# The first unit of a fused attention and MoE kernel under a fixed engine order

## The chip, the cores and the metric

One of the eight cores of a Trainium2 chip runs the whole program. The metric is device time in microseconds (us) from the start to the end of one execution; lower is better. Below, PE is TensorE (PEld its weight loads), DVE is VectorE, ACT is ScalarE, POOL is GpSimd, SP is SyncE, and L12 is line 12 of the kernel's file.

## What is computed

Three stages follow each other on 4608 tokens: an attention through 32 packed queries per head, a dense MLP with squared ReLU, and a routed MLP of eight experts.

```python
def _attn_ref(q, k, v, p):                 # q, k, v: 8 x 8 x 576 x 64, p: 8 x 8 x 32 x 64
    p_packed = sm_attn(p, k, v)            # packs: softmax(p k^T) v
    return sm_attn(q, p_packed, p_packed)  # the tokens attend to the packs

def _moe_ref(x, w_in, w_out):              # w_in 512 x 2048, w_out 2048 x 512, given as float64 words
    h = np.maximum(x @ w_in, 0.0)
    return h * h @ w_out

def _moe2_ref(x, modality_id, w_gate, modality_bias, w1, w2):
    logits = x @ w_gate + modality_bias[modality_id]
    ...                                    # each token goes to its best expert, scaled by its gate
```

## The kernel before

**The pack phase** (steps `i` = 0 to 18 of a loop written out under `tc.manual_schedule()`, so that every engine takes its instructions in the written order). Step `i` works on quad `i`, four heads of a batch: `scores(i)` on PE, `greatest(i)` (maximum on DVE, exponential on ACT), `normalise(i)`, then two steps later the transposes (`turn_a`, `turned_a`), and three steps later `values(i - 3)` and `packs(i - 3)`. `packs` reads the result `pq` out of PSUM twice, on DVE into `pp32` (the operand of the tokens' attention) and on ACT into `ppq` (a compact copy), in turn for each half. Beside it run, one piece per step, the conversion of the float64 weights (`conv_in` for w_in, four DVE instructions and one ACT square per block; `conv_out` for w_out, which also halves the result into a high and a low part on ACT and POOL), `turn_p` on POOL, which makes the left operand of `scores` two batches ahead, and from step 11 the quads `pw_quad`: the packs times w_in, two matmuls of 64 rows each, copied out of PSUM into `pws` and written to `pw_d` in DRAM. One quad is 512 KB. Sixteen of the 32 are made in the steps, for batches 0 to 3. `att2(0)`, the attention of the first 384 tokens, runs in nine pieces in steps 10 to 18.

**The units.** The tokens go through the dense MLP in twelve units of 384 tokens. Unit `u` loops over 16 blocks `f` of the hidden width: `layer1` (6 matmuls into `ph`; ACT: ReLU, square, high part; the low part of `ghl` on POOL in unit 0 and on DVE later) and `layer2` of the block before (9 matmuls into `acc`). The left operand of `layer1` are blocks of `pw_d`, loaded (`load_pw`, into `praw`) and halved by `split_pw` on ACT and POOL into `head` and `ring`. Unit 0 carries more (`others`): the other 16 quads, `conv_out` of the last 12 blocks of w_out, and `att2(1)`; the constants of the routing (`setup_routing`, some 30 small POOL instructions and two small loads) also belong to it in the code. Unit 1 begins with `tail(0)`, the router's dot products of unit 0 on DVE.

**What sets the order.** Only the pack phase stands under the manual schedule. From there on a scheduler orders each engine's instructions by its own estimate of when they can run, and it may lift an instruction of a later part above the end of the pack phase. All loads and some of the writes are issued by SP, in order; writes of `pws` copied by ACT in the pack phase are issued by ACT. PSUM is eight banks; `pws` has three buffers, `praw` two.

Of the kernel before, what the change touches and what calls it, by code (L numbers as in the profile page):

```python
# [26 lines left out]
def tile_pack_attention_moe_moe2(  # L27
# [880 lines left out]
    with tc.manual_schedule():  # L908
# [58 lines left out]
        for w in (2, 3):
            split_pw(0, w - 1)
            for _ in conv_out(w):
                pass  # L970
        split_pw(0, 3)
    st2.close()
    ps0.close()
    held.pop("early")
# [150 lines left out]
```

## Time and profile before

| | us |
|---|---|
| median of 3 runs | 1281.64 (1280.64 to 1284.12) |
| the profiled execution, its own time | 1284.8 |
| its span, first to last instruction | 1282.9 |
| PE busy in the span | 1214.0 (95%) |
| DVE busy | 835.7 (65%) |
| ACT busy | 637.6 (50%) |
| POOL busy | 293.7 (23%) |
| mean granted TensorE clock | 0.985 |

Busy shares are means over the whole span. A stage is read from a window of its own, from the timeline (start, duration, engine, line, operation, what it writes and reads, and in brackets the idle time of the engine before it and what ended that idle time), and from groups of instructions within a window.

### The profile page before, as it was taken

How to read it: one execution, taken by the hardware profiler on the slowest of the kernel's cores; microseconds unless marked ns; L12 is line 12 of the kernel's file. 1: busy time of each engine (PE TensorE's matmuls, PEld its weight loads, DVE VectorE, ACT ScalarE, POOL GpSimd, SP SyncE). 2: the span in 40 equal slices, each digit the busy share in tenths (PEclk: the TensorE clock that was granted, in tenths of full speed). 3: DMA queues.
4: the chain of work that ended last, by engine and by line, in shares of the span. 5: the costliest groups of instructions: out<-in, count | busy, mean ns of one | idle time of the engine just before them, and what ended most of it. 6: DMA issues, size and time to landing. Idle time of an engine off the chain costs nothing.

```text
span 1282.9 us, 17702 instructions
## 1 busy us (share of the span) xinstructions
PE 1214.0 (95%) x6036; PEld 982.3 (77%) x6036; DVE 835.7 (65%) x2145; ACT 637.6 (50%) x1328; POOL 293.7 (23%) x353
## 2 busy tenths in 40 slices
PE   6886799999999999999999998999999999999995
PEld 4653456788888888888888887878788888888884
DVE  5766964968767984878778497878653354354331
ACT  4664564676546766466755576632332343243220
POOL 5013733322103232013320033101221122032011
PEclk8998899999999999999999999999999999999998
DMA  9988754221111212112110112341442452353210
GB/s 338 366 331 270 225 201 158 64 75 66 35 42 50 75 50 67 43 30 87 59 58 17 51 51 76 103 145 68 157 156 91 150 182 94 121 193 116 88 66 35
DMA packets 75316, 149.20 MB, mean 116 GB/s; under 512 B 5712, under 2 KB 25296, under 8 KB 75088
## 3 DMA queue, kind: packets, MB, share of 16 engines
q1 hardware_dynamic: 66464, 123.04, 28.5%
q0 software_dynamic: 5760, 19.17, 4.6%
q10 hardware_dynamic: 2992, 5.77, 1.2%
q8 instruction: 49, 0.80, 0.3%
q14 instruction: 51, 0.42, 0.1%
HBM read 112.01 MB, written 35.95 MB: 115 GB/s over the span
## 4 chain that ended last, share of the span: by engine, by line
PE 71%; DVE 15%; DMA 6%; ACT 3%; issue 3%; POOL 2%; ACTq 0%; POOLq 0%; SPq 0%; DVEq 0%
PE acc L519 23%; PE h L809 15%; PE o L831 15%; PE ph L493 9%; DVE rows L540 5%; PE pw L376 2%; DMA wraw<-in_moe_w 2%; PE s L444 2%; DVE r L506 1%; PE tr L789 1%; DVE ghl L512 1%; DMA wgb<-in_k 1%; DMA pw_d<-pws 1%; PE pq L354 1%; DMA early<-in_v 1%
## 5 line engine op out<-in xcount | busy, mean ns | idle before, releaser
L519 PE MATMUL acc<-wb,ghl 128*128 128x512 f32 x1728 | 445.8, 400 | 9.5 <-ACT ghl L510 8.3
L519 PEld LDWEIGHTS acc<-wb,ghl 128*128 128x128 f32 x1728 | 318.6, 189 | 81.3 <-ACT ghl L510 11.3
L540 DVE SCALAR_TENSOR_TENSOR rows<-rows,wgb 128x512 f32<-128x512 f32 x288 | 213.8, 742 | 3.6
L809 PE MATMUL h<-xt,wb 128*128 128x512 f32 x864 | 213.9, 397 | 0.5 <-DVE ht L820 0.5
L809 PEld LDWEIGHTS h<-xt,wb 128*128 128x128 f32 x864 | 162.3, 188 | 39.8 <-DVE ht L820 1.0
L512 DVE TENSOR_TENSOR ghl<-r,ghl 128x384 fp32r<-128x384 f32 x176 | 106.5, 606 | 72.6 <-ACT ghl L510 72.3
L510 ACT ACTIVATE ghl<-r 128x384 fp32r<-128x384 f32 x192 | 99.9, 522 | 76.3 <-PE acc L519 74.1
L820 DVE SCALAR_TENSOR_TENSOR ht<-h,ht 128x512 fp32r<-128x512 f32 x72 | 49.0, 687 | 115.7 <-ACT ht L819 115.7
L831 PE MATMUL o<-head,ht 128*128 128x512 f32 x432 | 114.3, 399 | 4.1 <-ACT ht L819 3.9
L842 POOL DMA_INDIRECT out<-wgb,idx_s x36 | 36.7, 1020 | 342.6 <-DVE wgb L840 253.2
L819 ACT ACTIVATE ht<-h 128x512 fp32r<-128x512 f32 x72 | 42.3, 593 | 144.7 <-PE h L809 144.5
L831 PE MATMUL o<-ring,ht 128*128 128x512 f32 x432 | 112.5, 395 | 0.0
L509 ACT ACTIVATE r<-r 128x384 f32<-128x384 f32 x192 | 100.2, 523 | 4.4
L831 PEld LDWEIGHTS o<-head,ht 128*128 128x128 f32 x432 | 80.6, 189 | 23.7 <-ACT ht L819 5.0
L415 POOL TENSOR_TENSOR ring<-praw,ring 128x256 fp32r<-128x256 f32 x70 | 62.1, 892 | 155.8 <-ACT ring L414 150.3
L508 ACT ACTIVATE r<-ph 128x384 f32<-128x384 f32 x128 | 61.9, 485 | 65.5 <-PE ph L493 37.5
L831 PEld LDWEIGHTS o<-ring,ht 128*128 128x128 f32 x432 | 80.1, 188 | 16.8
L467 POOL TENSOR_TENSOR e<-e,sm 128x256 f32<-128x256 f32 x36 | 36.0, 1000 | 228.3 <-DVE sm L466 158.9
L493 PE MATMUL ph<-a2T,ring 128*128 128x384 f32 x420 | 87.3, 341 | 0.0
L493 PEld LDWEIGHTS ph<-a2T,ring 128*128 128x128 f32 x420 | 74.2, 188 | 9.0 <-issue 3.0
L493 PE MATMUL ph<-a2T,head 128*128 128x384 f32 x348 | 73.4, 345 | 3.7 <-ACT head L414 2.8
L415 POOL TENSOR_TENSOR head<-praw,head 128x256 fp32r<-128x256 f32 x58 | 51.4, 888 | 105.0 <-ACT head L414 105.0
(199 smaller groups left out, 1727.9 us busy)
## 6 DMA issues: line engine op xcount, KB each, us to landing
wraw<-in_moe_w SPq DMA_DIRECT2D x72, 512.0 KB, 3.7
praw<-pw_d SPq DMA_DIRECT2D x32, 512.0 KB, 3.7
pw_d<-pws SPq DMA_DIRECT2D x21, 512.0 KB, 3.9
x_d<-rows SPq DMA_DIRECT2D x12, 792.0 KB, 3.6
qT<-in_q SPq DMA_DIRECT2D x36, 256.0 KB, 2.9
early<-in_v SPq DMA_DIRECT2D x16, 512.0 KB, 9.4
stage<-in_moe_w_in SPq DMA_DIRECT2D x16, 512.0 KB, 9.0
rows<-in_k SPq DMA_DIRECT2D x10, 576.0 KB, 8.5
```

The source lines that it names most:

```text
L415: nc.gpsimd.tensor_tensor(out=t[:, 1], in0=raw, in1=t[:, 0].bitcast(F32), op=ALU.subtract)
L493: nc.tensor.matmul(ph, t[:, x, c, :], a[:, y, c, :], start=(i == 0), stop=(i == 3 * NPC - 1))
L508: nc.scalar.activation(out=r, in_=ph if len(ps) == 1 else r, func=AF.Relu)
L509: nc.scalar.activation(out=r, in_=r, func=AF.Square)
L510: nc.scalar.activation(out=hl[:, 0], in_=r, func=AF.Copy)
L512: eng.tensor_tensor(out=hl[:, 1], in0=r, in1=hl[:, 0].bitcast(F32), op=ALU.subtract)
L519: nc.tensor.matmul(acc[t], hl[:, x, t * P : (t + 1) * P], w_out_block(f)[:, y, :], start=(f == 0 and x == 0 and y == 0), stop=(f == NF - 1 ...
L540: nc.vector.scalar_tensor_tensor(out=junk, in0=row[:, t, :DM], scalar=1.0, in1=wgb[:, e], op0=ALU.mult, op1=ALU.mult, accum_out=one)
L809: nc.tensor.matmul(ph, half1(g, c)[:, x, f * P : (f + 1) * P], xs[c][:, y, :], start=(i == 0), stop=(i == 3 * NDC - 1),)
L819: nc.scalar.activation(out=h[:, 0, :], in_=ph, func=AF.Relu)
L820: nc.vector.scalar_tensor_tensor(out=h[:, 1, :], in0=ph, scalar=0.0, in1=h[:, 0, :].bitcast(F32), op0=ALU.max, op1=ALU.subtract)
L831: nc.tensor.matmul(po, hs[f][:, x, t * P : (t + 1) * P], second(f)[:, y, :], start=(i == 0), stop=(i == 3 * NFE - 1),)
```

## The change

The whole of unit 0 moves into the manual schedule: its loop over `f` is now written out there (first layer of `f`, second layer of `f - 1`, halves of w_out block `f + 2`, conversion of block `f + 3`, one quad, the split of block `f + 3`, loads, one piece of `att2(1)`), and the scheduler begins with unit 1. `conv_out` is cut in two (`conv_out`, `halve_out`). `packs` keeps only the DVE copies; `compact`, one step later, makes the ACT copies from `pp32` in SBUF. `att2(0)` starts at step 4 instead of 10 and has five pieces per 128 tokens instead of three. Five more quads stand between the pack phase and unit 0, and one in each of the first 11 blocks of unit 0; the two matmuls of a quad always stand next to each other. `setup_routing` stands in step 3, and the first two loads of q in steps 2 and 3 instead of 6 and 7.

```diff
     def conv_out(u):
...
         yield from convert(m, tf, raw)
+        load_out(u + 3)
+
+    def halve_out(u):
+        tf = whole[u % 2]
         hi, lo = w_out_block(u)[:, 0], w_out_block(u)[:, 1]
         nc.scalar.activation(out=hi, in_=tf, func=AF.Copy)
         nc.gpsimd.tensor_tensor(out=lo, in0=tf, in1=hi.bitcast(F32), op=ALU.subtract)
-        load_out(u + 3)
...
     def packs(i):
...
-            nc.vector.tensor_copy(pp32[js, b, gs, ns], src)
-            nc.scalar.activation(out=ppq[js, gs, b, :], in_=src, func=AF.Copy)
+            nc.vector.tensor_copy(pp32[js, b, 2 * qd : 2 * qd + 2, ns], src)
+
+    def compact(i):
...
+            nc.scalar.activation(out=ppq[js, gs, b, :], in_=pp32[js, b, gs, ns], func=AF.Copy)
...
+            if 4 <= i:
+                compact(i - 4)
...
-            if i in (6, 7):
-                qts[(i - 6) * P] = load_q((i - 6) * P)
-            if i >= 10:
+            if i in (2, 3):
+                qts[(i - 2) * P] = load_q((i - 2) * P)
+            if i == 3:
+                setup_routing(x2_p)
+            if i >= 4:
                 next(bg)
...
+        split_pw(0, 0)
+        halve_out(1)
+        cv = conv_out(2)
+        for w in range(5):
+            pw_next("ACT" if made % 2 else "DVE")
+            next(cv, None)
+            if w < 2:
+                split_pw(0, w + 1)
...
+        bg = att2(1, True)
+        pend = None
+        for f in range(NF):
+            hl = layer1(0, f)
+            if pend is not None:
+                if f == 1:
+                    held["acc"] = [bank("acc", "acc") for _ in range(UT)]
+                layer2(held["acc"], *pend)
+            pend = (f, hl)
+            if f + 2 < NU:
+                halve_out(f + 2)
+            if f + 3 < NU:
+                for _ in conv_out(f + 3):
+                    pass
+            pw_next(None)
+            if f + 3 < NF:
+                split_pw(0, f + 3)
+            if f in (0, 5):
+                load_pw(0, 2 + f // 5)
+            next(bg, None)
+            ahead(0, 0, f)
...
-    for u in range(NUN):
+    for u in range(1, NUN):
```

How it moves instructions, at three places (rows in an engine's order; L414 before is L422 after, L390 L398, L364 L372, L258 L262, L376 L384, L493 L505, L519 L531, L294 L297).

ACT between the pack phase and unit 0, before. `praw_1005` and `praw_1102` are the second and third loads of `pw_d`, `praw_944` the first, which block 0 needs; `ppq` is the last compact copy.

```order
L414 ACTIVATE head_1007<-praw_1005 128x256 x4
L364 ACTIVATE ppq_87<-pq_1017 64x2x32 x2
L477 ACTIVATE a2T_592<-ta2_1032 128x2x128
L390 ACTIVATE pws_1046<-pw_1043 128x1024
L393 DMA pw_d_134<-pws_1046 128x2x512
L414 ACTIVATE ring_1098<-praw_1102 128x256 x4
L390 ACTIVATE pws_1058<-pw_1055 128x1024
L393 DMA pw_d_134<-pws_1058 128x2x512
L414 ACTIVATE head_1007<-praw_944 128x256
```

The same place after; `praw_988` is the first load.

```order
L262 ACTIVATE wb0_1057<-tf_89 128x512
L489 ACTIVATE a2T_354<-ta2_1019 128x2x128
L398 ACTIVATE pws_1084<-pw_1081 128x1024
L401 DMA pw_d_134<-pws_1084 128x2x512
L398 ACTIVATE pws_1096<-pw_1093 128x1024
L401 DMA pw_d_134<-pws_1096 128x2x512
L372 ACTIVATE ppq_87<-pp32_85 64x2x32 x2
L422 ACTIVATE head_1048<-praw_988 128x256
```

The eight splits of the second and third load, which stood ahead of the first load's, are gone from there; they now come in the order of the blocks, inside unit 0.

PE in unit 0, before, around its third block: the two matmuls of a quad (`pw_1268` and `pw_1269`, `pw_1276` and `pw_1277`) have others between them.

```order
L376 MATMUL pw_1268<-wi5_113,ppq_87 128x512
L493 MATMUL ph_1301<-a2T_592,head_1007 128x384 x2
L376 MATMUL pw_1269<-wi5_113,ppq_87 128x512
L493 MATMUL ph_1301<-a2T_592,head_1007 128x384
L376 MATMUL pw_1276<-wi5_113,ppq_87 128x512
L493 MATMUL ph_1301<-a2T_592,head_1007 128x384 x2
L493 MATMUL ph_1344<-a2T_592,head_1007 128x384 x6
```

After, the first two blocks of unit 0.

```order
L384 MATMUL pw_1147<-wi5_113,ppq_87 128x512 x2
L505 MATMUL ph_1164<-a2T_354,head_1048 128x384 x6
L384 MATMUL pw_1184<-wi5_113,ppq_87 128x512
L384 MATMUL pw_1185<-wi5_113,ppq_87 128x512
L452 MATMUL s2_1197<-pp32_85,qT_1101 128x64 x4
L505 MATMUL ph_1210<-a2T_354,head_1048 128x384 x6
L531 MATMUL acc_1221<-wb0_1057,ghl_1163 128x512 x2
```

Each block is now one run of `ph`, one of `acc` and one whole quad.

POOL in steps 2 to 5, before: `ptb_120` and `ptb_121` are the operands of even and odd batches, written by `turn_p`; `idt` is the load of the modality numbers.

```order
L294 TENSOR_SCALAR ptb_120<-pn_119 64x4x32 x2
L294 TENSOR_SCALAR ptb_121<-pn_119 64x4x32 x2
L189 CAST idf_1783<-idt_1781 128x36
L197 TENSOR_SCALAR is1_1787<-idf_1783 128x36
L198 TENSOR_TENSOR bias_all_93<-is1_1787,mb_1785 128x288
```

After.

```order
L189 CAST idf_296<-idt_294 128x36
L197 TENSOR_SCALAR is1_300<-idf_296 128x36
L198 TENSOR_TENSOR bias_all_93<-is1_300,mb_298 128x288
L197 TENSOR_SCALAR is1_300<-idf_296 128x36
L198 TENSOR_TENSOR bt_301<-is1_300,mb_298 128x288
L204 TENSOR_TENSOR bias_all_93<-bias_all_93,bt_301 128x288
L297 TENSOR_SCALAR ptb_121<-pn_119 64x4x32 x2
```

The operand of batch 3, which `scores(6)` reads, stood ahead of the wait for `idt`; now it stands behind it. From unit 2 on, the orders are those of before but for a few neighbours exchanged.

## Rows read from the trace of the kernel before

**Rows 1.** Page, part 2: DMA rate in 40 slices of 32.07 us.

```profile
GB/s 338 366 331 270 225 201 158 64 75 66 35 42 50 75 50 67 43 30 87 59 58 17 51 51 76 103 145 68 157 156 91 150 182 94 121 193 116 88 66 35
```

**Rows 2.** Windows: us, busy us of each engine (instructions), clock, DMA share, GB/s.

```profile
core 0: us, PE busy (x) PEld busy (x) DVE busy (x) ACT busy (x) POOL busy (x), PEclk, DMA share, GB/s
100.00:120.00 20.00, 11.74 (x62) 6.30 (x62) 8.87 (x17) 8.16 (x17) 4.79 (x6) 0.86 0.77 240
140.00:160.00 20.00, 15.05 (x49) 8.88 (x49) 18.51 (x24) 9.63 (x20) 15.35 (x13) 0.83 0.71 225
82.60:126.10 43.50, 29.20 (x165) 17.15 (x165) 27.55 (x55) 22.61 (x45) 9.32 (x11) 0.92 0.77 267
126.10:228.30 102.20, 92.98 (x358) 57.40 (x359) 67.79 (x96) 56.17 (x115) 53.45 (x47) 0.95 0.58 191
228.30:291.50 63.20, 60.99 (x328) 51.83 (x327) 48.25 (x133) 45.86 (x116) 19.36 (x23) 1.00 0.22 70
```

**Rows 3.** Timeline between the pack phase and unit 0.

```profile
113.94 1.33 ACT L414 ACTIVATE head<-praw 128x256 fp32r<-128x256 f32 x4 [3.60 <-DMA praw<-pw_d]
115.41 0.23 DVE L363 COPY pp<-pq 64x64 f32<-64x64 f32 x1 [6.45 <-ACT ppq L364]
117.94 5.39 PE L376 MATMUL pw<-wi,ppq 64*128 64x512 f32 x14 [7.13 <-DVE pws L392]
122.07 1.34 ACT L414 ACTIVATE ring<-praw 128x256 fp32r<-128x256 f32 x4 [4.85 <-DMA praw<-pw_d]
126.10 0.62 PE L493 MATMUL ph<-a2T,head 128*128 128x384 f32 x2 [2.77 <-ACT head L414]
```

**Rows 4.** Timeline of the pack phase: `idt`, `turn_p`, scores of quads 6 and 15, values.

```profile
24.89 0.59 POOL L189 CAST idf<-idt 128x36 f32<-128x36 int32 x1 [4.68 <-DMA idt<-in_moe_modality_id]
29.22 1.90 POOL L294 TENSOR_SCALAR ptb<-pn 64x128 f32<-64x128 f32 x2
31.71 1.19 PE L307 MATMUL s<-wgb,ptb 128*64 128x288 f32 x8
71.19 2.50 PE L354 MATMUL pq<-atbuf,early 128*128 128x128 f32 x20 [0.68 <-ACT ppq L364]
82.64 1.19 PE L307 MATMUL s<-wgb,ptb 128*64 128x288 f32 x8 [1.05 <-ACT abuf L319]
```

**Rows 5.** DMA issues, line engine xcount, KB each, us to landing, 0:60 and 80:126.

```profile
idt<-in_moe_modality_id SPq DMA_DIRECT2D x1, 36.0 KB, 8.0
pw_d<-pws ACTq DMA_DIRECT2D x9, 512.0 KB, 5.4
```

**Rows 6.** Timeline of unit 0: a paired quad, one block, and its evacuation.

```profile
172.26 1.13 PE L376 MATMUL pw<-wi,ppq 64*128 64x512 f32 x4
188.63 1.32 PE L493 MATMUL ph<-a2T,ring 128*128 128x384 f32 x6
189.79 2.25 PE L519 MATMUL acc<-wb,ghl 128*128 128x512 f32 x9
228.34 0.68 DVE L530 COPY rows<-acc 128x512 f32<-128x512 f32 x1
```

**Rows 7.** Groups in 118:226: xcount, busy us, mean ns, idle before.

```profile
L376 PE MATMUL pw<-wi,ppq 64*128 64x512 f32 x72 | 35.2, 735 | 9.4 <-DVE pws L392 7.1 <-ACT pws L387 1.2 <-DVE pws L388 0.9
L227 DVE SCALAR_TENSOR_TENSOR tf<-sq,tf 128x512 f32<-128x512 f32 x15 | 13.2, 881 | 0.5 <-ACT sq L211 0.2
L219 DVE SCALAR_TENSOR_TENSOR tf<-wgb,tf 128x512 int32<-128x512 int32 x10 | 11.8, 1182 | 0.1
L215 DVE TENSOR_SCALAR tf<-wgb 128x512 int32<-128x512 int32 x9 | 7.8, 861 | 4.2 <-POOL wb L259 4.2
L388 DVE COPY pws<-pw 128x512 f32<-128x512 f32 x16 | 11.0, 685 | 15.5 <-PE pw L376 15.5
```

**Rows 8.** Two lines to 235 us: ns min/median/max of one instruction.

```profile
L219 DVE SCALAR_TENSOR_TENSOR wi<-stage,wi x16: 640/686/728, 12.7 to 97.9; 128x512 int32<-128x512 int32 x16
L259 POOL TENSOR_TENSOR wb<-tf,wb x16: 1264/1286/1790, 109.9 to 220.3; 128x512 fp32r<-128x512 f32 x16
```

More of the change, by code (lines that the diff above doesn't have):

```diff
@@ L360, in packs @@
         for j in range(2):
+            js, ns = slice(j * D, (j + 1) * D), slice(j * NPK, (j + 1) * NPK)
+            src = pq[js, : 2 * own].rearrange("p (g x) -> p g x", g=2)[:, :, ns]
+            nc.vector.tensor_copy(pp32[js, b, 2 * qd : 2 * qd + 2, ns], src)
+    def compact(i):
+        b, qd = quads[i]
+        for j in range(2):
             js, ns, gs = slice(j * D, (j + 1) * D), slice(j * NPK, (j + 1) * NPK), slice(2 * qd, 2 * qd + 2)
-            src = pq[js, : 2 * own].rearrange("p (g x) -> p g x", g=2)[:, :, ns]
-            nc.vector.tensor_copy(pp32[js, b, gs, ns], src)
-            nc.scalar.activation(out=ppq[js, gs, b, :], in_=src, func=AF.Copy)
+            nc.scalar.activation(out=ppq[js, gs, b, :], in_=pp32[js, b, gs, ns], func=AF.Copy)
     def pw_quad(bq, u, eng):
@@ L432, in load_q, with att2 @@
         return qT
-    def att2(u):
+    def att2(u, fine=False):
         hl = held["at"].tile([P, 2, NPC, UW], F32R, tag="a2T", name="a2T", bufs=2)
@@ L450, in att2 @@
                     )
-            if u == 0 and r + 2 < UT:
+            if fine and r + 2 < UT:
                 qts[t0 + 2 * P] = load_q(t0 + 2 * P)
@@ L918, in tile_pack_attention_moe_moe2, with pw_next @@
         turn_p(1)
-        bg = att2(0)
-        cv, nxt, made = None, None, 0
+        bg = att2(0, True)
+        cv, made = None, 0
+        def pw_next(eng):
+            nonlocal made
+            if made < 2 * NU:
+                pw_quad(*divmod(made, NU), eng)
+                made += 1
         for i in range(NQ + 3):
@@ L954, in tile_pack_attention_moe_moe2 @@
                 load_out(i - 13)
-            if i in (6, 7):
-                qts[(i - 6) * P] = load_q((i - 6) * P)
-            if i >= 10:
+            if i in (2, 3):
[3 more added lines that the diff above has]
+            if i >= 4:
                 next(bg)
             for _ in range({16: 3, 17: 4, 18: 4}.get(i, 1 if i >= 11 else 0)):
-                pw_quad(0, made, "ACT" if i < 16 or made % 2 else "DVE")
-                made += 1
+                pw_next("ACT" if i < 16 or made % 2 else "DVE")
@@ L962, in tile_pack_attention_moe_moe2 @@
             if i in (16, 17):
                 load_pw(0, i - 16)
-        split_pw(0, 0)
+        compact(NQ - 1)
+        for t in range(2):
+            qts[UW + t * P] = load_q(UW + t * P)
         for _ in cv:
             pass
[L967 to L974, printed above, removed]
-    held["all"] = ctx.enter_context(tc.tile_pool(name="ps", bufs=2, space=PSUM, reuse_waits="tile"))
@@ new lines, in tile_pack_attention_moe_moe2 @@
+        halve_out(1)
+        cv = conv_out(2)
+        for w in range(5):
+            pw_next("ACT" if made % 2 else "DVE")
+            next(cv, None)
+            if w < 2:
+                split_pw(0, w + 1)
+        for _ in bg:
+            pass
+        st2.close()
+        ps0.close()
+        held.pop("early")
+        held["all"] = ctx.enter_context(tc.tile_pool(name="ps", bufs=2, space=PSUM, reuse_waits="tile"))
+        held["ring"] = const.tile([P, RING - HEAD, 2, NPC, P], F32R, tag="ring", name="ring")
@@ L1011, in background @@
         return gens, n
-    pend = None
+    pend = (0, *pend)
     def second_layer():
```

37 lines of the change are left out of this document (12 added, 25 removed).

## Prediction

> **What bounds the kernel now.** I read the DMA rates over the span first [rows 1]. The first three slices move 331 to 366 GB/s, then the rate falls and stays low: the kernel is bound by loads for about 96 us, and by PE later. The orders agree from unit 2 on, so only the time up to the end of unit 1 is in question. I cut it by the windows [rows 2] at three events. Scores of quad 15 start at 82.64 [rows 4]. The first `layer1` of unit 0 starts at 126.10 [rows 3]. Unit 0's sums leave PSUM at 228.34 [rows 6]. Between 82.6 and 126.1 PE works 29.2 of 43.5 us; in unit 0 it works 93.0 of 102.2 us at a mean clock of 0.95; in unit 1 61.0 of 63.2 us. So unit 1 is full already, and what can be won lies between 82.6 and 228.3 us.
>
> The timeline ahead of unit 0 [rows 3] names the loss. At 113.94 ACT starts four splits after 3.60 us of waiting for a load of `pw_d`, and these stand ahead of the last compact copy. DVE's second pack copy waits 6.45 us for that copy, and PE stands 7.13 us until `pws` is copied. At 122.07 ACT waits 4.85 us for the next load, before the split that PE needs; PE starts at 126.10. That is an order in which later work waits in front of earlier work.
>
> **The change part by part.**
>
> *Steps 0 to 15.* `values` at 71.19 waited 0.68 us for ACT's compact copy [rows 4]. With both copies of PSUM on DVE that wait goes. The ACT copies cost the same from SBUF, in ACT's idle time; if they were in the way they would cost their own 0.4 us a step. The finer `att2(0)` adds no instruction, only earlier ones. Against this stands `setup_routing`. Before, POOL began on `idt` at 24.89 after 4.68 us of waiting, needed 4.33 us for the constants (29.22 - 24.89), and had made batch 3's operand before [rows 4]; scores of quad 6 ran at 31.71. Now `idt` is issued at about 27 us (step 3, behind one more load of q) and lands 8.0 us later [rows 5], at 35. POOL is done with the constants at 39.3, the operand takes up to 1.9 us [rows 4], so quad 6 starts at about 41: nine us late. Behind POOL's wait stand `turn_p(3)`, `turn_p(4)` and the first `att2` multiplication. The loads run on from what is queued, since a load takes 8 us to land. From 31.71 to 82.64 before, nine steps took 5.66 us each, the last ones longest. PE's own work in a step is the transposes, scores of 1.19, values of 2.50, and from step 11 a quad of 1.13 [rows 4, 6]: I estimate 4.1 us without and 5.15 us with a quad. From 41, five steps of 4.1 and four of 5.15 give 82.1. So I take 82, as before: the stall is bought back, not more. Bounds: 77, if `idt` lands as early as before, and 88, if steps stay as slow as before.
>
> *From quad 15's scores to unit 0.* The order rows show the splits of later blocks gone from here, so the waits at 113.94 and 122.07 go. Late next is DMA: 43.5 us at 267 GB/s are 11.6 MB, and about the same must move now (the writes of quads 2 to 15, the last loads of v and w_out, two loads of `pw_d`). When busy, the engines moved 240/0.77 = 312 GB/s in 100 to 120 us and 267/0.77 = 347 in the whole window [rows 2]; that is 33.4 to 37.2 us. Five quads more stand ahead of unit 0 on PE, 5 x 1.13 = 5.7 us, but their matmuls run while earlier writes land; what counts is that the last waits for a `pws` buffer, and a write lands in 5.4 us [rows 5], three at a time, 1.8 us each. Sixteen quads from step 16 on then take 29 us, which is below the bytes. I take 37, nearest to the window with the most writes: unit 0 starts at 82 + 37 = 119, 7.1 us earlier than 126.1. Bounds 33 and 43.5.
>
> *Unit 0.* In 118 to 226 us, 72 records of `pw`, 18 quads, took 35.2 us, 1.96 each [rows 7]; the paired one at 172.26 took 1.13 for its four records [rows 6]. Before, 16 quads of unit 0 cost 31.3 us; now 11 cost 12.4. PE's work falls from 93.0 to 74.1 us, at the old clock. The clock was 0.83 in 140 to 160, where PE idled 5 of 20 us [rows 2]; with PE busier I expect 1.00, which makes the floor about 71. The other limit is DVE. A block has four conversions, 0.86, 1.18, 0.88 and, for the one not shown, 0.87, and a copy of 0.69 [rows 7]: 4.48 us; the pieces of `att2(1)` I put at 0.5 a block, the overlap of neighbours at -0.1. I take 4.9 for the 11 blocks with a quad, above PE's 188.63 to 189.79 plus 2.25 plus 1.13 = 4.5 [rows 6]; 4.1 for two blocks with conversion alone; 3.45 for the last three. 53.9 + 8.2 + 10.4 + 3.0 to the evacuation = 75.5 us, against 102.2: 26.7 us less. Bounds: 71, PE alone, and 92.
>
> POOL has three instructions a block; 53.45 us over 47 is 1.14 each [rows 2], so 3.4 of 4.9 us. ACT has seven of about 0.5. Each queue has its wait on another: PE's `acc` of block f - 1 waits for POOL's low part, behind which stand two more POOL instructions and PE's next quad; one block of distance, 4.9 us, covers that chain of ReLU, square, high and low part.
>
> *Unit 1 on.* Same work, same order but for its beginning: nothing. The gate weights are loaded behind the last conversion, three blocks ahead of their use.
>
> The sum: 7.1 + 26.7 = 33.8 us. The profiled execution took 1284.8, so 1251.0; it lies 3.2 above the median of the three runs, 1281.64, so on the median 1247.8. **Forecast 1248 us.**
>
> **The rivals.**
>
> *The order ties the engines together (slower).* Place: unit 0. If a block's chain does not overlap the next, it costs PE 1.2 + 2.2 + 1.1, ACT 1.5 for the three of `ghl`, POOL 1.1, the copy 0.6 and a split with its POOL part 1.4, about 9 us. Eleven blocks at 9 instead of 4.9 are +45 us: 1293. It decides from 4.9 + 33.8/11 = 8.0 us a block. For it: every engine now takes its instructions in one written order, and each wait holds up all that stands behind it. Against it: the written order leaves one block between maker and user everywhere. Chance 0.04.
>
> *DVE and POOL stop each other.* One conversion took 0.69 us in the pack phase, where POOL is idle, and 1.18 in unit 0 [rows 7, 8]; DVE and POOL were busy 18.5 and 15.4 of 20 us [rows 2], so part of that is waiting. If all of a block's conversions (four, at most 0.69 alone: 2.5 us) exclude its POOL work (three of about 1.0 alone; the low half takes at least 1.26 [rows 8]) and the copy and `att2` come on top, a block takes 2.5 + 3.0 + 0.7 + 0.5 = 6.7 us: 11 x 1.8 = +20, 1268. The Trainium skill, "SBUF — State Buffer", section "Who interferes with whom", states that a VectorE instruction with two SBUF inputs and a GpSimd instruction that reads SBUF exclude each other for the whole instruction. The lengthening in rows 7 and 8 agrees in kind; that it is always so, no row shows. Chance 0.13.
>
> *The start is not won.* POOL's wait for `idt` is not made up (88 at quad 15) or the writes take as long as before (43.5): +6 each, 1254 to 1260. For it: the DMA share was 0.77, not 1. Chance 0.13.
>
> *More is won.* `idt` lands early, steps 4 to 15 gain from the freed PSUM, unit 0 runs at PE's 71 us: -5 - 4.5, 1238. Chance 0.07.
>
> *The change does nothing there.* The order rows exclude that the splits or pairs stay as they were; a delay that stems from elsewhere and leaves the time as it was: 0.03.
>
> **How the numbers follow.** The forecast has 0.60, with a range of its own from 1240 to 1257. Range for 8 in 10: 1235 to 1268, which takes in the better case, the late start and most of the DVE case, and leaves out the slower one. A change of under 0.3%, 3.8 us, can't be told from none. Faster: 0.60 + 0.13 + 0.13 + 0.07 = 0.93; same 0.03; slower 0.04.
>
> **What would show it.** Right: PE starts `layer1` of unit 0 at 115 to 123 us, without ACT waiting for `praw`; every `pw` quad in unit 0 takes 1.1 us; block to block 4.5 to 5.2 us; evacuation near 194; clock 1.00 in unit 0; unit 1 again 63 us. The POOL wait would show as PE idle before quad 6 with `turn_p` as its releaser. Wrong: a block pitch above 6 us (then DVE's instructions of two inputs are long, or PE waits for `ghl`), a start after 123 (then DMA or `idt`), or unit 1 longer than before, which would give the gain back where DVE is busy with the router.

## The result

The changed kernel takes 1267.24 us in the median (1266.85 to 1269.01), the kernel before 1281.14 us beside it: ratio 0.9892, 95% interval 0.9871 to 0.9913, so 13.9 us less. A second series of the changed kernel (experiment 18) gave 1268.67 us and 0.9902 (0.9886 to 0.9919). The direction was right, and the time lies in the range, at its upper end. The forecast was 1248, a gain of 33.8 us, of which 13.9 came.

The same cuts as in the prediction, in the profiled execution after (1266.85 us, span 1265.0). The DMA rates (40 slices of 31.6 us) and the windows answer to [rows 1, 2]; columns as there:

```profile
GB/s 345 325 369 302 228 221 158 52 76 64 30 43 51 76 59 51 43 51 76 51 60 43 35 43 102 110 116 111 117 184 94 124 201 108 94 201 130 73 67 36
core 0: us, PE busy (x) PEld busy (x) DVE busy (x) ACT busy (x) POOL busy (x), PEclk, DMA share, GB/s
86.40:128.12 41.72, 32.08 (x169) 17.21 (x168) 27.42 (x50) 21.22 (x38) 5.38 (x6) 0.91 0.90 308
128.12:143.12 15.00, 15.00 (x51) 11.12 (x52) 10.07 (x15) 8.84 (x18) 7.00 (x6) 0.68 0.83 274
128.12:216.14 88.02, 81.05 (x353) 60.59 (x354) 69.94 (x94) 57.10 (x118) 59.08 (x51) 0.89 0.60 206
216.14:277.69 61.55, 59.10 (x319) 50.80 (x318) 45.66 (x129) 43.75 (x111) 19.45 (x22) 1.00 0.22 68
```

| stretch | before | forecast | after | forecast missed by |
|---|---|---|---|---|
| start to scores of quad 15 | 82.64 | 82 | 86.40 | 4.4 |
| from there to unit 0 ("tail") | 43.5 | 37 | 41.7 | 4.7 |
| unit 0, to its evacuation | 102.2 | 75.5 | 88.0 | 12.5 |
| unit 1, evacuation to evacuation | 63.2 | 63.2 | 61.6 | -1.7 |

The four misses sum to 19.9 us, all of the shortfall: 33.8 - 13.9. So unit 0 gave 14.2 us, the tail and unit 1 1.7 us each, and the start lost 3.8. The spans of the two profiled executions differ by 17.9 us; the other 4.1 lie behind unit 1 (991.4 us before, 987.3 after), where no edit of the experiments reaches and the profiled executions differ all the same (987.1 to 995.3 us). The one of before was 3.2 us above its median.

**The start.** POOL and PE in the timeline (answers to [rows 4]):

```profile
28.78 1.94 PE L452 MATMUL s<-pp,qT 128*128 128x64 f32 x8 [5.00 <-DMA qT<-in_q]
33.84 3.23 PE L357 MATMUL pq<-atbuf,early 128*128 128x128 f32 x20
35.61 0.22 POOL L189 CAST idf<-idt 128x36 f32<-128x36 int32 x1 [15.39 <-DMA idt<-in_moe_modality_id]
39.32 2.77 POOL L297 TENSOR_SCALAR ptb<-pn 64x128 f32<-64x128 f32 x4
40.95 1.19 PE L310 MATMUL s<-wgb,ptb 128*64 128x288 f32 x8 [3.33 <-POOL ptb L297]
42.07 4.13 PE L357 MATMUL pq<-atbuf,early 128*128 128x128 f32 x20
```

`idt` lands at 35.6, quad 6 starts at 40.95: as forecast (35, and 41). The first matmuls of `att2(0)` (L452) also wait 5.00 us, for their q load. `values` behind the two waits takes 3.23 and 4.13 instead of 2.50 us; the granted clock was 0.83 in 20 to 40 us and 0.91 in 40 to 60.

**The tail.** The longest waits of ACT and DVE between 86.4 and 128.1 us (line waited for, us, times, longest):

```profile
ACT pws L398 <- DMA pw_d<-pws: 11.7, 4, 6.1
DVE pws L400 <- DMA pw_d<-pws: 6.6, 3, 4.5
```

No split waits for `praw` any more, where [rows 3] showed 3.60 and 4.85 us. In its place the copies of `pw` wait 18.3 us for a free `pws` buffer, that is for writes to `pw_d`.

**Unit 0.** Every quad is paired; seven of the eleven take 1.13 us, the others 1.31 to 2.08, the longest in block 0. PE stands still twice, and DVE and POOL show why. In time order:

```profile
169.11 1.48 POOL L263 TENSOR_TENSOR wb<-tf,wb 128x512 fp32r<-128x512 f32 x1
169.47 1.67 DVE L219 SCALAR_TENSOR_TENSOR tf<-wgb,tf 128x512 int32<-128x512 int32 x1
170.56 1.18 POOL L423 TENSOR_TENSOR ring<-praw,ring 128x256 fp32r<-128x256 f32 x1
171.18 1.11 DVE L223 SCALAR_TENSOR_TENSOR tf<-wgb,tf 128x512 int32<-128x512 int32 x1
172.33 1.13 PE L384 MATMUL pw<-wi,ppq 64*128 64x512 f32 x4
172.39 0.69 DVE L227 SCALAR_TENSOR_TENSOR tf<-sq,tf 128x512 f32<-128x512 f32 x1
173.00 0.68 DVE L396 COPY pws<-pw 128x512 f32<-128x512 f32 x1
173.60 0.60 DVE L474 TENSOR_REDUCE sm<-e 128x8 f32<-128x256 f32 x1
174.73 0.83 POOL L477 TENSOR_TENSOR e<-e,sm 128x256 f32<-128x256 f32 x1 [2.99 <-DVE sm L476]
175.62 0.69 PE L484 MATMUL ta<-ident,e 128*128 128x128 f32 x2 [2.16 <-POOL e L477]
...
193.48 1.21 PE L505 MATMUL ph<-a2T,ring 128*128 128x384 f32 x6
198.72 1.03 DVE L227 SCALAR_TENSOR_TENSOR tf<-sq,tf 128x512 f32<-128x512 f32 x1
199.67 0.60 DVE L474 TENSOR_REDUCE sm<-e 128x8 f32<-128x256 f32 x1
201.59 0.69 PE L484 MATMUL ta<-ident,e 128*128 128x128 f32 x2 [4.81 <-POOL e L477]
216.14 0.68 DVE L542 COPY rows<-acc 128x512 f32<-128x512 f32 x1
```

Windows, columns as above, and DVE's longest wait in unit 0:

```profile
146.11:189.60 43.49, 41.33 (x185) 28.65 (x184) 41.93 (x52) 30.25 (x62) 33.12 (x27) 0.96 0.61 209
201.59:207.94 6.35, 6.35 (x25) 5.71 (x26) 0.87 (x3) 2.12 (x5) 3.83 (x4) 0.65 0.71 292
DVE tf L227 <- ACT sq L211: 5.3, 3, 3.4
```

From block 2's copy (146.11) to block 10's (189.60) DVE has hardly a gap: 41.9 of 43.5 us, 5.4 us a block. In blocks 0 to 2 it had waited 5.3 us for ACT's squares, which stand behind the ReLU of the same block; PE's first two blocks take 6.0 us each there, at a granted clock of 0.50 (its lower level, 1.2 GHz) and 0.69, against 4.4 for block 2. DVE's two-input conversions take 0.69 us when POOL has paused (172.39) and 1.1 to 1.7 us beside POOL's `wb` and `ring`. The sum of `att2(1)` stands behind them, POOL's multiplication waits for the sum, PE's transposes wait for POOL. At 193.48 PE begins block 13, which has no conversion, but DVE ends block 12's at 199.75: it has fallen 6 us behind, and PE loses 4.81 us to that. Half of the lag, 3.1 us, comes in blocks 11 and 12, which have a conversion but no quad: PE needs 3.2 us for each, DVE 4.7. Behind the wait, up to block 15, the granted clock is 0.65 and PE works 6.35 us.

The groups of DVE's conversions in unit 0 (128 to 216 us) answer to [rows 7]:

```profile
L227 DVE SCALAR_TENSOR_TENSOR tf<-sq,tf 128x512 f32<-128x512 f32 x13 | 14.6, 1127 | 6.3 <-ACT sq L211 5.3
L223 DVE SCALAR_TENSOR_TENSOR tf<-wgb,tf 128x512 int32<-128x512 int32 x9 | 11.1, 1232 | 0.3
L219 DVE SCALAR_TENSOR_TENSOR tf<-wgb,tf 128x512 int32<-128x512 int32 x9 | 11.0, 1223 | 0.3
```

### The profile page after: what moved, and what is told of

It reads as the page before. It is cut to its first block, busy times and chain, and to the rows that moved or that the text cites. A ratio compares the mean times of both kernels' runs of the same rounds, so it can differ in the third digit from the quotient of the medians.

```text
span 1265.0 us, 17700 instructions
## 1 busy us (share of the span) xinstructions
PE 1206.9 (95%) x6036; PEld 987.4 (78%) x6036; DVE 838.7 (66%) x2143; ACT 637.8 (50%) x1325; POOL 298.2 (24%) x353
## 4 chain that ended last, share of the span: by engine, by line
PE 76%; DVE 12%; DMA 6%; issue 3%; POOL 2%; ACT 2%; SPq 0%; POOLq 0%; DVEq 0%; ACTq 0%
PE acc L531 23%; PE h L821 15%; PE o L843 15%; PE ph L505 10%; DVE rows L552 4%; PE pq L357 2%; PE s L452 2%; DMA wraw<-in_moe_w 2%; PE pw L384 2%; DMA early<-in_v 2%; DMA pw_d<-pws 1%; DVE r L518 1%; PE tr L801 1%; PE s L310 1%; DVE ghl L524 1%
## 5 line engine op out<-in xcount | busy, mean ns | idle before, releaser
L531 PE MATMUL acc<-wb,ghl 128*128 128x512 f32 x1728 | 442.6, 399 | 2.6 <-ACT ghl L522 2.2
L531 PEld LDWEIGHTS acc<-wb,ghl 128*128 128x128 f32 x1728 | 321.3, 190 | 64.0 <-ACT ghl L522 4.3
L821 PEld LDWEIGHTS h<-xt,wb 128*128 128x128 f32 x864 | 161.8, 188 | 40.1 <-DVE ht L832 1.6
L505 PE MATMUL ph<-a2T,ring 128*128 128x384 f32 x420 | 87.9, 346 | 0.0
L505 PEld LDWEIGHTS ph<-a2T,ring 128*128 128x128 f32 x420 | 75.9, 192 | 5.7 <-issue 1.5
L423 POOL TENSOR_TENSOR head<-praw,head 128x256 fp32r<-128x256 f32 x58 | 52.8, 911 | 111.2 <-ACT head L422 101.8
L505 PE MATMUL ph<-a2T,head 128*128 128x384 f32 x348 | 74.3, 349 | 1.4 <-DVE pws L400 1.4
```

What stands on the lines that cost most here:

```text
L423: nc.gpsimd.tensor_tensor(out=t[:, 1], in0=raw, in1=t[:, 0].bitcast(F32), op=ALU.subtract)
L505: nc.tensor.matmul(ph, t[:, x, c, :], a[:, y, c, :], start=(i == 0), stop=(i == 3 * NPC - 1))
L531: nc.tensor.matmul(acc[t], hl[:, x, t * P : (t + 1) * P], w_out_block(f)[:, y, :], start=(f == 0 and x == 0 and y == 0), stop=(f == NF - 1 ...
L821: nc.tensor.matmul(ph, half1(g, c)[:, x, f * P : (f + 1) * P], xs[c][:, y, :], start=(i == 0), stop=(i == 3 * NDC - 1),)
```

## The experiments

All but the last are the changed kernel with the edit shown; times are medians, ratios to the kernel before on the same chip.

**1. `idt` loaded early.** POOL's wait at the start, taken away.

```diff
     def setup_routing(sp):
...
-        nc.sync.dma_start(idt, ...)
+        idt, mb = early_ids
...
-        nc.sync.dma_start(
-            mb, ...
...
         load_in(1)
+        idt = x2_p.tile([P, NTL, 2], I32, tag="idt", name="idt")
+        nc.sync.dma_start(idt, ...)
...
+        early_ids = idt, mb
         turn_p(0)
```

> The loads of idt and of the router's bias are issued ahead of the pack loop, the constants are still worked out in step 3. If POOL's wait for idt is what holds scores of quad 6 (40.95 us, 3.33 us of PE idle), quad 6 starts by about 35 and the gain stays: quad 15 at 81 to 83 instead of 86.4, 1262 to 1264 in all. If the loads of q, k and v set the pace of the steps (PE also waited 5.00 us for the q load at 28.78), quad 6 starts earlier but quad 15 does not: 1266 to 1268.

1267.0 us, 0.9873 (0.985 to 0.9896): no difference from the changed kernel that can be told. Quad 6 starts at 38.05 us, 2.9 us earlier but not by the 35 that I had written: quad 5 starts at 33.19, behind 5.68 us of waiting for the q load. Quad 15 starts at 81.86 us, 4.5 us earlier. From 38.05 to 59.59 five steps take 4.3 us each, from there to quad 15 four take 5.6. But unit 0 starts at 126.60, 1.5 us earlier only: the tail grew by most of what the start had won.

```profile
81.86:126.60 44.74, 32.88 (x170) 17.27 (x169) 28.00 (x51) 21.09 (x38) 5.52 (x6) 0.89 0.88 302
```

So POOL's wait and the slow `values` behind it delay quad 15, but little of that reaches unit 0 in this execution, since the tail runs 3 us longer at 302 GB/s: 13.5 MB.

**2. The five quads of the tail in unit 0.**

```diff
         for w in range(5):
-            pw_next("ACT" if made % 2 else "DVE")
             next(cv, None)
...
-            pw_next(None)
+            for _ in range(2 if f in (1, 3, 5, 7) else 1):
+                pw_next(None)
```

> The five pw quads of the tail go into unit 0 (blocks 1, 3, 5 and 7 get two). If the tail is bound by the writes of pw (DVE and ACT waited 18.3 us for free pws buffers), it shortens by 5 x 1.7 us = 8 us at most, to 34 to 37 us, and unit 0 grows by 5 x 1.1 us of PE work plus what DVE and ACT take for the copies, so 93 to 97 us: 1263 to 1270. If the tail is bound by something else (the loads, the conversions) it stays at 41 and the time rises to 1273 to 1277.

1266.26 us, 0.9868 (0.9842 to 0.9895).

```profile
86.69:120.13 33.44, 24.04 (x150) 14.93 (x149) 23.16 (x45) 17.52 (x33) 2.02 (x2) 0.95 0.87 294
120.13:214.98 94.85, 87.12 (x373) 61.61 (x374) 74.57 (x100) 61.87 (x127) 62.30 (x55) 0.91 0.64 221
```

The tail is 8.3 us shorter, as five times 1.7 us of writes asks (512 KB each, at 308 GB/s); it moves 294 x 33.44 = 9.8 MB where the changed kernel moves 308 x 41.72 = 12.8. Unit 0 takes 6.8 us more. So the tail is set by its writes. Whether by their bytes or by the wait for one of three `pws` buffers, this edit doesn't separate.

**3. The piece of `att2(1)` first in each block**, ahead of halves, conversion, quad and split.

```diff
             pend = (f, hl)
+            next(bg, None)
             if f + 2 < NU:
...
-            next(bg, None)
             ahead(0, 0, f)
```

> In each block of unit 0 the piece of att2(1) stands ahead of the conversion, the halves, the quad and the split instead of behind them. If PE's two stalls at the transposes of att2 (7.0 us, and slow matmuls after each) come from DVE being late with its sums behind four conversions, both go and unit 0 falls from 88 to 78 to 82 us: 1258 to 1262. If DVE is simply full, PE stalls elsewhere in the block instead: 1265 to 1269.

1265.05 us, 0.9862 (0.9836 to 0.9887). Unit 0 takes 83.0 us instead of 88.0, PE's wait for POOL's multiplication 1.0 us in all instead of 7.0; 2.4 us of waiting for DVE's copies of `pw` came in. From these transposes to block 15:

```profile
202.06:207.11 5.05, 4.58 (x25) 3.85 (x26) 4.14 (x5) 2.64 (x6) 5.05 (x4) 1.00 0.42 149
```

PE works 4.58 us there at a granted clock of 1.00, instead of 6.35 at 0.65: the late wait had cost its own length and 1.8 us of slower matmuls behind it. This execution began unit 0 at 132.51 us, so most of the 5 us doesn't show in the time; the spread of that start is taken up in experiment 18.

**4. The low halves of w_out on DVE instead of POOL.**

```diff
-        nc.gpsimd.tensor_tensor(out=lo, in0=tf, in1=hi.bitcast(F32), op=ALU.subtract)
+        nc.vector.tensor_tensor(out=lo, in0=tf, in1=hi.bitcast(F32), op=ALU.subtract)
```

> The low half of each w_out block moves from POOL to DVE. If DVE and POOL shut each other out while both read SBUF, DVE's conversions shorten (1.2 towards 0.7 us) and the 0.7 us that DVE takes on costs nothing or less: 1258 to 1267. If the two engines run beside each other and DVE is full by itself, the fourteen halves add 14 x 0.7 = 10 us to unit 0: 1272 to 1278.

1269.97 us, 0.9895 (0.9873 to 0.9917): no difference that can be told. In unit 0 (129.51 to 215.92) DVE has 14 instructions more:

```profile
129.51:215.92 86.41, 77.95 (x350) 57.21 (x349) 70.07 (x108) 56.89 (x117) 35.58 (x36) 0.93 0.63 210
L263 DVE TENSOR_TENSOR wb<-tf,wb 128x512 fp32r<-128x512 f32 x14 | 11.5, 821 | 4.5 <-ACT wb L262 4.1
L227 DVE SCALAR_TENSOR_TENSOR tf<-sq,tf 128x512 f32<-128x512 f32 x13 | 10.2, 787 | 1.4
L223 DVE SCALAR_TENSOR_TENSOR tf<-wgb,tf 128x512 int32<-128x512 int32 x9 | 8.3, 925 | 0.3
L219 DVE SCALAR_TENSOR_TENSOR tf<-wgb,tf 128x512 int32<-128x512 int32 x9 | 8.0, 891 | 0.3
```

DVE's busy time is 70.07 us with 108 instructions, 69.94 with 94: the 11.5 us that came in went out of the conversions (1.13, 1.23 and 1.22 to 0.79, 0.93 and 0.89 us). POOL's fell from 59.1 to 35.6. So the two engines do hold each other up. The first case that I had written was right about durations, wrong about the time: unit 0 was 1.6 us shorter, no more than executions of the same unit 0 differ by (experiment 18), and unit 1 was that much longer.

**5. Quads unpaired.** acc's matmuls between the two halves of a quad: `next(quad)` makes the first half, the loop over `quad` the second, the copies and the write.

```diff
             hl = layer1(0, f)
+            if made < 2 * NU:
+                quad = pw_quad(*divmod(made, NU), None, True)
+                made += 1
+                next(quad)
             if pend is not None:
...
                 layer2(held["acc"], *pend)
...
-            pw_next(None)
+            for _ in quad:
+                pass
```

> In blocks 1 to 10 of unit 0 the two halves of a pw quad stand on either side of acc's nine matmuls instead of side by side. If pairing is worth what the durations say (1.13 us for a pair, 1.1 us for each half alone), PE gets ten times 1.1 us more and, as it worked 81 of 88 us there, unit 0 takes 96 to 99 us: 1275 to 1279. If DVE sets the pace of these blocks, PE has the room and unit 0 stays below 92: 1267 to 1271.

1274.68 us, 0.9939 (0.9919 to 0.9959), 6 to 7 us above the changed kernel. The profiled execution was the longest of ten (1282.1); in it PE was busy 97.5 of 100.8 us of unit 0, whose first 15 us went at a granted clock of 0.50, so that its length is in part the clock's. By the medians pairing is worth 6 to 7 us here, about six tenths of ten times 1.1: with the pairs apart PE sets the pace, with them together DVE does for most blocks.

**6. PE kept busy in the tail.** Six products that nobody reads.

```diff
+        def fill():
+            nc.tensor.matmul(bank("t", "fill"), ident, wi[7][:, HP - 1], start=True, stop=True)
...
         for w in range(5):
+            fill()
             pw_next("ACT" if made % 2 else "DVE")
...
+        fill()
         for _ in bg:
```

> Six products that nobody reads (1.1 us each) are put on PE ahead of the last five quads and of unit 0, where PE waits for pws copies. If the low clock of unit 0's first 15 us (0.68) comes from PE's idle time in the tail, the clock there rises to 0.85 or more and unit 0 shortens by 4 to 6 us: 1261 to 1264. If it does not, these products only delay the quads: the clock stays below 0.75 and the time is 1267 to 1270.

1269.61 us, 0.9905 (0.987 to 0.994).

```profile
129.25:144.25 15.00, 15.00 (x70) 10.79 (x71) 12.25 (x15) 12.38 (x25) 10.99 (x9) 1.00 0.87 290
129.25:216.83 87.58, 77.19 (x353) 58.02 (x354) 72.42 (x93) 56.98 (x118) 58.07 (x51) 0.92 0.59 207
```

The clock of the first 15 us rose from 0.68 to 1.00, and the first three blocks took 12.0 us instead of 16.4. But unit 0 took 87.6 us, as before: PE waited 10.4 us for `att2` (three times, from block 3 on) instead of 7.0. The clock there is 1.00 in both executions with such products in the tail (this one and number 12), 0.89 and 0.90 where they stand behind the quads (numbers 17 and 9), 0.50 to 0.89 without them. What the clock won here, PE waited for later. My first theory, that slow matmuls at its start lengthen unit 0, falls here.

**7 and 8. Edits 1 to 3 together; and with 4.**

> The three edits together: loads of idt and bias ahead of the loop, the five quads of the tail in unit 0, att2(1)'s piece first in each block. If the tail of 41.7 us was bound by the bytes of the quads, both of the first two now count: quad 15 at 82, unit 0 from 115 to 118 and, with 6.8 us more for the five quads and 5.0 us less for the stalls, 90 us long: 1253 to 1258. If something else (DVE, loads) holds the tail, unit 0 starts at 120 again and the time is 1260 to 1264.

> As the run before, and the low halves of w_out on DVE. With these halves on DVE the conversions shortened to 0.79 to 0.93 us and DVE's busy time in unit 0 did not grow. If POOL's lower load (59 to 36 us) matters once the stalls at att2 are gone, the time is 2 to 4 us below the run before; if DVE's queue is what counts, it is 0 to 3 us above.

1262.0 us, 0.984 (0.9807 to 0.9873), and 1261.57, 0.9839 (0.9808 to 0.9871). With the tail free of the five writes, the early `idt` counts: unit 0 starts at 115.89 and 115.38 us, where number 2 had 120.13. It takes 92.5 and 91.8 us, more than I wrote. The halves on DVE again make no difference that can be told. From the start of the program to unit 0, in the changed kernel, in number 2 and in number 7:

```profile
0.00:128.12 128.12, 102.80 (x642) 69.65 (x642) 87.90 (x208) 69.96 (x140) 28.78 (x57) 0.93 0.96 335
0.00:120.13 120.13, 92.29 (x623) 65.17 (x623) 83.28 (x203) 66.08 (x135) 24.53 (x53) 0.94 0.95 333
0.00:115.89 115.89, 91.08 (x622) 64.24 (x622) 83.25 (x203) 65.73 (x135) 25.15 (x53) 0.95 0.98 346
```

The DMA engines are busy 0.95 to 0.98 of all this time and move 42.9 MB with the five quads, 40.0 and 40.1 without. That speaks for the bytes as what sets the start of unit 0; the early `idt` shows as a higher rate.

**9 and 12. The unread products again**, in number 8 (between the last quad and unit 0), and in number 3.

> As the run with three edits and the low halves on DVE, and six unread products on PE (1.1 us each) between the last quad and unit 0, where PE stood still for 4.1 to 6.9 us. There PE was busy 89.8 of 91.8 us of unit 0 at a mean clock of 0.91, and 0.70 in its first 15 us. If PE at its granted clock now bounds unit 0, the first 15 us go at 0.9 or more and unit 0 takes 86 to 88 us: 1256 to 1259. If DVE is still the limit, PE's time becomes waiting, unit 0 stays at 91 and the time is 1261 to 1264.

> att2(1)'s piece first in each block and the six unread products in the tail, nothing else. The pieces first alone left PE busy 79.1 of 83.0 us in unit 0 at a clock of 0.94, 0.78 in its first 15 us; the products alone brought that to 1.00, and PE then waited for att2 instead. If both causes are what I hold them for, unit 0 takes 77 to 80 us with PE busy 75 of it, and the time is 1262 to 1265 (the tail is 2 us longer). If DVE is the limit once the clock is up, unit 0 stays at 82 to 84: 1266 to 1269.

Number 9: 1266.16 us (1259.3 to 1268.2), 0.9893 (0.9873 to 0.9913): slower than number 8, and outside both of my ranges. Its profiled execution, the fastest of six, took unit 0 down to 89.2 us, so this is not read from unit 0; why the others were longer stays open. Number 12: 1268.0, 0.9893 (0.9868 to 0.9918); unit 0 83.3 us at a first clock of 1.00, against 83.0 at 0.78 without the products. That is the second case that I had written, DVE as the limit.

**10 and 11. Two parts of the change undone**: `att2(0)` coarse and from step 10, with its q loads in steps 6 and 7, as before; and ACT's compact copies from PSUM, right behind DVE's.

```diff
-        bg = att2(0, True)
+        bg = att2(0)
...
-            if i in (2, 3):
-                qts[(i - 2) * P] = load_q((i - 2) * P)
+            if i in (6, 7):
+                qts[(i - 6) * P] = load_q((i - 6) * P)
...
-            if i >= 4:
+            if i >= 10:
                 next(bg)
```

```diff
             nc.vector.tensor_copy(pp32[js, b, 2 * qd : 2 * qd + 2, ns], src)
+            nc.scalar.activation(out=ppq[js, 2 * qd : 2 * qd + 2, b, :], in_=src, func=AF.Copy)
...
-            if 4 <= i:
-                compact(i - 4)
...
-        compact(NQ - 1)
```

> att2(0) as before: nine pieces from step 10 on, q loads in steps 6 and 7; all else as in the changed kernel. If the early start costs what PE waits for q at 28.78 us (5.00 us), quad 6 starts earlier by up to 5 us, unless idt is the later of the two, and the pieces now lie in steps 10 to 18 that are bound by writes: 1265 to 1268. If the finer pieces win in steps 10 to 18, the time rises to 1270 to 1274.

> ACT's compact copies read PSUM again, right behind DVE's pack copies, in place of SBUF a step later. If they matter, values wait for ACT in each step as at 71.19 us before (0.68 us) and the steps from 6 to 15 take 0.3 to 0.7 us more, 3 to 7 us, of which the tail, bound by writes, takes back most: 1268 to 1272. If PE's wait there is hidden: 1266 to 1268.

The first: 1271.84 us, 0.9928 (0.9905 to 0.9951), 3 to 5 us above the changed kernel, with intervals that touch. Quad 15 came 1.9 us earlier (84.46) and the tail took 47.0 us. Where no piece of `att2(0)` stands, from quad 7 to quad 10 (44.96 to 57.24 us), a step takes 4.1 us. The second: 1275.22 us, 0.995 (0.993 to 0.997), 7 to 8 us slower. PE waits for ACT's copies again, as [rows 4] showed at 71.19:

```profile
PE pq L357 <- ACT ppq L367: 3.0, 4, 1.1
```

That is the sum from 45 to 92 us; the changed kernel has no wait there. Quad 15 starts at 91.23, 4.8 us later, and the tail (45.2 us) took nothing back, against what I had written. The waits make 3.0 of the 4.8 us; the rest wasn't traced.

**13 and 14. One copy of each quad from DVE to ACT in unit 0**, alone, and with edits 1 and 3.

```diff
             nc.scalar.activation(out=so[:, 0], in_=ph[0], func=AF.Copy)
-            nc.vector.tensor_copy(so[:, 1], ph[1])
+            nc.scalar.activation(out=so[:, 1], in_=ph[1], func=AF.Copy)
```

> In unit 0 both copies of a pw quad go to ACT; one of 0.68 us was DVE's. If DVE's stream bounds unit 0, the eleven copies are 7.5 us of it: the stall at 201.59 us (4.81) goes, unit 0 takes 80 to 83 us, 1260 to 1263. If PE's clock or POOL's chain bounds it, 86 to 88 and 1266 to 1268. If ACT (57 of 88 us busy, now 63) comes late with ReLU and splits, it gets longer: over 1269.

> The same with the early loads of idt and bias and with att2(1)'s piece first in each block; the five quads stay in the tail. By the bytes the tail takes 42 to 45 us from quad 15 at 82. If DVE and the stalls at att2 were two limits of unit 0, it falls to 77 to 80: 1257 to 1261. If they were one and the same, 81 to 83 as with the pieces first alone: 1262 to 1265.

Number 13: unit 0 took 83.2 us, as DVE's theory asks, though the stall that I expected to go stayed (5.22 us at 200.43). It began at 131.52, and the time is 1268.0 us, 0.9892 (0.9857 to 0.9928): no gain that can be told. Number 14: 1259.62 us, 0.9827 (0.9811 to 0.9843).

```profile
126.64:141.64 15.00, 15.00 (x56) 10.87 (x56) 10.60 (x15) 10.96 (x22) 8.29 (x7) 0.75 0.71 224
126.64:205.73 79.09, 76.36 (x355) 56.40 (x356) 67.86 (x84) 61.80 (x130) 60.42 (x51) 0.95 0.70 228
```

Unit 0 takes 79.1 us and PE works 76.4 of them.

The two edits act on two places. Split where PE begins block 13, the first without a conversion (193.48 in the changed kernel):

| kernel | clock, first 15 us | blocks 0 to 12 | to the evacuation |
|---|---|---|---|
| forecast | | 62.1 | 13.4 |
| changed kernel | 0.68 | 65.4 | 22.7 |
| the same again (18) | 0.89 | 64.9 | 23.2 |
| 6, unread products | 1.00 | 64.3 | 23.3 |
| 4, low halves on DVE | 0.84 | 64.2 | 22.2 |
| 3, piece first | 0.78 | 65.2 | 17.8 |
| 12, piece first, products | 1.00 | 65.5 | 17.8 |
| 13, copy on ACT | 0.84 | 60.4 | 22.8 |
| 14, both | 0.75 | 60.1 | 19.0 |

Less work on DVE shortens the blocks with conversions by 5 us; the earlier place of the sum shortens the end by 4 to 5 us; the clock of the first 15 us changes neither.

**15 to 17. The copy on ACT with edits 1 to 3; with 4 too; and 15 with five unread products.**

> The same with the five quads in unit 0 too. Before (three edits) PE worked 89.4 of 92.5 us there at a clock of 0.91. If PE's own work and clock bound it now, DVE's relief brings 0 to 2 us: 1260 to 1262. If DVE still held it up (blocks of 7 to 10 us early on), 3 to 6 us: 1256 to 1259.

> The same with w_out's low halves on DVE, where 0.7 us a block comes in for the 0.7 that went out, and POOL has one instruction less. If DVE's conversions shorten again by what POOL no longer does, this is the fastest: 1255 to 1259. If PE bounds it, it equals the run before.

> As e15_three_act, with five unread products of 1.1 us on PE between the last quad and unit 0, where PE stood 5.30 us. If the clock there costs time now that PE is busy 84.4 of 85.4 us, the first 15 us go at 0.9 or more, unit 0 takes 81 to 83 and the time is 1251 to 1254. If another engine takes over, as with the same products before (DVE or ACT late with the copies of pw), 85 again and 1255 to 1258; if the products delay unit 0 itself, up to 1260.

1255.81 us, 0.9794 (0.9778 to 0.981); 1258.61, 0.9807 (0.9791 to 0.9824); 1259.48, 0.9823 (0.9808 to 0.9838). The first is the fastest kernel of all: 26.9 us below the kernel before, 11 to 13 below the changed one. Unit 0 starts 12.7 us earlier than in the changed kernel and is 2.6 us shorter with five quads more:

```profile
81.91:115.42 33.51, 25.14 (x149) 15.08 (x148) 23.57 (x46) 17.30 (x33) 2.02 (x2) 0.89 0.92 317
115.42:200.83 85.41, 84.40 (x375) 59.93 (x376) 63.40 (x85) 69.39 (x144) 60.41 (x55) 0.94 0.73 245
```

Here PE is the bound, 84.4 of 85.4 us. In number 16, which I had thought might be the fastest, unit 0 took 88.2 us: no gain from the halves on DVE here either. With the products of 17 PE's busy time there fell to 82.0, but it waited for copies of `pw` instead, and unit 0 was 1.0 us shorter and began 2 us later. Of the 4.3 us by which its profiled execution is longer than that of 15, 3.3 lie behind unit 1, where the two kernels are the same.

**18. The changed kernel again.**

> The changed kernel, unchanged. 1266 to 1269 in the median as the first time, 10 to 14 us above e15_three_act. If the 128.12 us at which unit 0 began in its first profile is the early end of a spread, it begins at 129 to 132 now and unit 0 is 2 to 4 us shorter for it, since DVE's stream sets its end; if the spread belongs to the edits, 128 and 88 us again.

1268.67 us. Unit 0 began at 129.85 us and took 88.07:

```profile
85.86:129.85 43.99, 31.89 (x169) 17.06 (x169) 27.90 (x50) 21.20 (x38) 5.83 (x6) 0.92 0.88 297
129.85:144.85 15.00, 15.00 (x64) 10.63 (x65) 11.32 (x14) 11.15 (x23) 9.74 (x9) 0.89 0.76 246
129.85:217.92 88.07, 78.48 (x353) 59.10 (x354) 72.04 (x93) 57.00 (x118) 58.45 (x51) 0.90 0.59 203
```

So the tail of one program varies by 2 us and more (41.7 and 44.0; 43.5 to 44.9 in numbers 3, 5 and 13, whose code is the same up to there), and unit 0 began between 128.1 and 132.5 us in these five. Unit 0 isn't shorter for a late start, as I had thought it might be. Single profiles can't settle differences of 2 us in that stretch, so the 1.5 us of experiment 1 at unit 0's start may be up to 5.9. Unit 0's own length repeats within 0.1 us in the two executions; in numbers 1, 6, 10 and 11, where its code is the same, it was 86.9 to 88.8.

## Why the prediction was wrong

- **Steps 0 to 15 (82, measured 86.4).** The late `idt`, the place of the wait and quad 6 at 41 us were right. What failed is the length of the steps: 4.1 and 5.15 us against 4.6 and 5.6 measured ((64.12 - 40.95)/5, (86.40 - 64.12)/4). PE has no gap from 40.95 to 86.40 us; I had left the pieces of `att2(0)` out ("adds no instruction, only earlier ones"), though the edit puts 8 `s` matmuls (1.0 us together) and two transposes (0.4 us) per 128 tokens just there. They make 1.4 of the 1.7 us by which the last four steps are longer, and 1.4 in the first five, where the slow `values` behind PE's wait adds 1.6. With neither beside them, steps take the 4.1 us of the forecast (experiment 10). By itself this step mattered little: without POOL's wait quad 15 came 4.5 us earlier, and the time was 1267.0 us (experiment 1).
- **The tail (37, measured 41.7 and 44.0).** The waits for `praw` went as forecast, and DMA was what came next, near the rate that I took: 308 and 297 against 312 GB/s. The failed term is "about the same must move now": 12.8 and 13.1 MB against 11.6. Seventeen writes of `pws` started in the window, 8.9 MB of it; before, thirteen. I had counted the five extra quads as PE work (5.7 us, hidden); their price is 8.3 us of writes (experiment 2).
- **Unit 0 (75.5, measured 88.0).** The pairing worked in every block, and PE's own work came out: it is busy 76.4 us in experiment 14, against 74.1 forecast. Two terms failed. The first is 4.9 us for a block with conversions and a quad, from 4.48 + 0.5 on DVE: blocks 0 to 10 took 59.0 us, 5.4 each, against 53.9. The conversions alone are 4.06 us a block (52.8 us in 13 blocks) where the sum had 3.79, and DVE at work without a gap makes a block in 5.4. In blocks 0 and 1 PE was slow as well, at the low clock, but with that clock raised it only waited sooner (experiment 6). Blocks 11 and 12, put at DVE's 4.1 us, PE did in 3.2 and left DVE behind. The second is "3.45 for the last three, 3.0 to the evacuation", which took DVE to be done when PE reaches block 13. It was 6 us late, the sum stood behind it, and the end took 22.7 us instead of 13.4. Of those 9.3 us, the place of the sum accounts for 5 (experiment 3): 3.3 of waiting and 1.8 of slower matmuls behind the wait. About 4 us more are work of unit 1 (its first layers and a part of `att2(2)`) that PE does ahead of unit 0's last acc, as in the kernel before; I had left it out.
- **The rival of DVE and POOL** (chance 0.13, 6.7 us a block) was right in kind, not in size. Conversions and POOL's instructions lengthen each other (experiment 4), yet the blocks took 5.4. The Trainium skill, "SBUF — State Buffer", section "Who interferes with whom", says that VectorE with two SBUF inputs and GpSimd reading SBUF exclude each other; the trace agrees: 0.69 us alone, 1.67 beside POOL. Why POOL's time wasn't added in full, as the rival had it, no run here shows. That the time came out at this rival's 1268 is luck: unit 0 lost 12.5 us to the forecast, not 20, and the start and the tail lost the rest.
- **The start is not won** (1254 to 1260) named the right places: both came, 4.4 and 4.7 us instead of 6 each. Its reason for the tail, slow writes, was not the one; there were more of them.
- **Clock.** I expected 1.00 in unit 0 and it was 0.89. Raised in the first 15 us, it changed nothing, since PE had to wait for DVE anyway. Behind the late wait, where PE sets the time, its fall to 0.65 is 1.8 us of the end, and went with the wait (experiment 3).
- Right: `setup_routing`'s delay, no loss from the fixed order as such (blocks of 4.4 us, at PE's own pace, where DVE isn't late), and the compact copies from SBUF as a gain. I costed that at the wait alone; undoing it costs 7 to 8 us.

Open: why number 9 ran slower in the median than its unit 0 says, why the tail and the stretch behind unit 1 vary between executions, and why unit 1 is 1.7 us shorter than before.

## What to carry over

Cost an extra store on the path at bytes over the rate that the stage already runs at, not at its matmuls. A stage bound by DMA can also swallow what is won ahead of it: the 4.5 us of experiment 1 at quad 15 made no difference in the time that can be told, while with the five writes gone they were 4.2 us at unit 0. In a hand-written order, compare each engine's running sum with the one that it feeds at the point where its work ends, not only per block: DVE, half a microsecond a block over its forecast, showed in PE as one wait in block 8 and a long one in block 13, not as a wait in each block. A short reduction on a chain of three engines belongs ahead of the long bulk work of its block, not behind it.

## What I had not expected of the hardware

- Fourteen instructions of 0.82 us moved from POOL to DVE left DVE's busy time as it was (69.94 and 72.04 us in two executions without the move, 70.07 with it), while POOL's fell by 23.5.
- The granted clock of the same 15 us of the same program was 0.68 in one execution and 0.89 in another, with unit 0 at 88.02 and 88.07 us.
- From 60 to 87 us, when 3 of 18 large transfers issued were writes, DMA moved 383 GB/s; in the tail, where 17 of 25 were, 291 to 310 in executions of the same code. Which of the two, mix or waiting for buffers, makes the difference wasn't tried.
